# Expert stage of a fused attention and mixture-of-experts kernel: turning the gathered tokens with a DRAM scratch and VectorE block transposes in place of TensorE transposes

## The chip, the cores and the metric

One Trainium2 chip, one core of it. The time is that of the whole program on the device, in microseconds (us), and is the median of three runs. The engines are called as in the profile: PE is TensorE (PEld its weight loads), DVE is VectorE, ACT is ScalarE, POOL is GpSimd, SP is SyncE, which here issues the plain DMAs.

## The reference

Attention with keys and values averaged over groups of eight positions, followed by a mixture of eight experts of which each token uses one:

```python
k_p = k.reshape(B, H, Sp, 8, D).mean(axis=3)          # q, k, v: (8, 8, 576, 64) float32
v_p = v.reshape(B, H, Sp, 8, D).mean(axis=3)
attn = softmax(q @ k_p^T / sqrt(D));  attn_out = attn @ v_p
x = attn_out.transpose(0, 2, 1, 3).reshape(4608, 512)  # one row per token
logits = x @ w_gate + modality_bias[modality_id]       # (4608, 8)
e_idx = argmax(logits);  gate_w = softmax(logits)[e_idx]
for e in range(8):                                     # w1: (8, 512, 1024), w2: (8, 1024, 512)
    h = maximum(x[e_idx == e] @ w1[e], 0)
    out[e_idx == e] = gate_w * (h @ w2[e])
```

## The kernel before

The first part (up to about 195 us) computes the attention, writes each token's row to a DRAM table `xs`, and sorts the tokens by expert. A row of `xs` holds 512 numbers, the token's gate weight in column 512, and from column `RX` = 520 on one factor per head (8 of them) by which the 512 numbers have yet to be multiplied.

The second part works in slots of 256 tokens of one expert. There are `NSTAT` = 18 slots that always run (numbered s = 0 to 17 in the code; slot 5 of the title is s = 4), and more only if the experts' counts need them. Instructions are issued on each engine in the order in which the program writes them (`manual_schedule`).

While slot s is computed, slot s + 1 is prepared:

- `gather(s + 1, ...)`: two indirect DMAs on POOL fetch 128 token rows each into two of the four tiles `xg`. The transition into slot 17 fetches a third tile, `xe`, since the last slot there can hold 128 tokens more (its operand is `xw` and not one of the two `xhl`).
- `scale`: POOL multiplies the 512 numbers of each row by the head's factor (L153).
- `x_transposes`: four PE transposes per tile of 128 tokens put the 512 numbers on partitions, in PSUM tile `xt` (L168); ACT copies them to the high part of `xhl` in float32r (L170); DVE subtracts that from the original and writes the low part (L171). Products of float32 numbers are made from such high and low parts.

A slot has eight steps f = 0 to 7, one for each 128 columns of the hidden layer. Step f consists of

- `hidden(f)`, which calls `first_wide`: eight matmuls into PSUM tile `hp[f % 2]` (L188: high weights by high and low tokens, 512 columns; L191: low weights by high tokens, 256 columns). Then ACT copies half of `hp` to `ht` (L193), DVE adds the other half (L194), ACT makes `hh` = relu in float32r (L195), DVE makes the low part `hlo` (L197).
- `second(f - 1)`: the twelve matmuls of step f - 1 by w2 (L1248), from its `hh` and `hlo`, into `op`.
- `renew(f - 1)`: where the next slot has another expert, ACT (L136) and DVE (L139) split newly loaded weights into high and low parts; SP issues conditional loads of the weights of slot s + 2 (L126, L129; not moved where the expert stays the same). DVE's part and the loads are kept in the list `lag` and issued one or two steps later, between L195 and L197.

The last step ends with `close`: it issues the first matmuls of the next slot (`first_next`, which is step 0 of slot s + 1 and reads the high and low tokens of all its 256 columns), then `second(7)`. In step 0 of the next slot the outputs of the old one are multiplied by the gate weight (`evac`, L1219 on DVE, L1221 on ACT), and scattered to the output by POOL (L1225).

In the slots that matter here (s = 3 to 16), the gather is issued in step 0, `scale` in step 3, and `x_transposes` in step 5, with the third tile of the last transition in step 6:

```python
if f == (3 if EARLY_SLOTS <= s < NSTAT - 1 else 4) and nxt and not early:
    scale(s + 1, xg)
    ...
if f == (5 if EARLY_SLOTS <= s < NSTAT - 1 else 6) and nxt:
    x_transposes(s + 1, xg)
...
if f == NF - 1 and s != NSTAT - 2:
    close()
```

Of the kernel before, what the change touches and what calls it, by code (L numbers as in the profile page):

```python
# [9 lines left out]
F32 = mybir.dt.float32  # L10
# [5 lines left out]
ALU = mybir.AluOpType  # L16
# [6 lines left out]
P = 128  # L23
SLOT = 256
EARLY_GROUPS = 2
EARLY_SLOTS = 2
EXTRA = (128,)
OOB = 1 << 20


@with_exitstack
def kernel(
# [12 lines left out]
    nc = tc.nc  # L45
    ctx.enter_context(tc.manual_schedule(engines=ENGINES))
    B, H, S, HD = q.shape
    NTOK, D = out.shape
    E, _, FF = w1.shape
# [6 lines left out]
    NF = FF // P  # L56
    ND = D // P
    XW = D + 16
    RX = D + 8
    NSTAT = NTOK // SLOT  # L60
# [8 lines left out]
    dram = ctx.enter_context(tc.tile_pool(name="dram", bufs=1, space=bass.MemoryType.DRAM))  # L69
# [19 lines left out]
    xg = [cp.tile([P, XW], F32, name=f"xg{i}") for i in range(4)]  # L89
    gate = cp.tile([P, NT], F32, name="gate")  # L90
    tri = cp.tile([P, P], BF16, name="tri")
    xhl = [cp.tile([P, ND, 2, SLOT], F32R, name="xhl0")]
# [8 lines left out]
    sidx0 = cp.tile([P, 2 * EARLY_SLOTS], I32, name="sidx0")  # L101
    meta = cp.tile([1, 2 + 2 * (NSLOT + 1) + len(EXTRA)], I32, name="meta")
    meta0 = cp.tile([1, 1], I32, name="meta0")
# [10 lines left out]
    def load_regs(s, e_ap, c_ap):  # L114
        e = nc.values_load(e_ap, engines=SP_ENGINE, min_val=0, max_val=E - 1,
                           skip_runtime_bounds_check_because="a sum over at most one expert's index")
        c = None
        if c_ap is not None:
            c = nc.values_load(c_ap, engines=SP_ENGINE, min_val=0, max_val=1,
                               skip_runtime_bounds_check_because="a comparison's result")  # L120
        regs[s] = (e, c)
# [25 lines left out]
    def gather(s, idx, col, xgs, rows=NTOK):  # L147
        for tt in range(2):
            gather_tile(xgs[(2 * s + tt) % 4], idx, col + tt, rows)

    def scale_tile(x):
        xv = x[:, 0:D].rearrange("p (h d) -> p h d", h=H)
        nc.gpsimd.tensor_tensor(xv, xv, x[:, RX:RX + H].rearrange("p (h o) -> p h o", o=1).to_broadcast([P, H, HD]),  # L153
                                op=ALU.mult)

    def scale(s, xgs):
        for tt in range(2):
            scale_tile(xgs[(2 * s + tt) % 4])

    xw = None  # L160

    def x_transposes(s, xgs, tts=(0, 1)):
        ab = xhl[s % len(xhl)] if s != NSTAT - 1 else xw
        for tt in tts:
            x = xgs[(2 * s + tt) % 4] if tt < 2 else xgs[4]
            pt = ps_tr.tile([P, ND, P], F32, tag="tr", name=f"xt_{s}_{tt}")
            for d in range(ND):
                nc.tensor.transpose(pt[:, d, :], x[:, d * P:(d + 1) * P], ident)  # L168
            sl = slice(tt * P, (tt + 1) * P)
            nc.scalar.copy(ab[:, :, 0, sl], pt)  # L170
            nc.vector.tensor_sub(ab[:, :, 1, sl], pt, ab[:, :, 0, sl].bitcast(F32))  # L171
# [13 lines left out]
    def first_wide(f, ab, ph, t, hh, hlo, between=lambda: None):  # L185

        for d in range(ND):
            nc.tensor.matmul(ph, hl[f][:, 0, d * P:(d + 1) * P], ab[:, d, :, 0:SLOT],  # L188
                             start=(d == 0), stop=False)
        for d in range(ND):  # L190
            nc.tensor.matmul(ph[:, 0:SLOT], hl[f][:, 1, d * P:(d + 1) * P], ab[:, d, 0, 0:SLOT],  # L191
                             start=False, stop=(d == ND - 1))
        nc.scalar.copy(t, ph[:, SLOT:2 * SLOT])  # L193
        nc.vector.tensor_add(t, t, ph[:, 0:SLOT])  # L194
        nc.scalar.activation(hh, t, AF.Relu)  # L195
        between()
        nc.vector.scalar_tensor_tensor(hlo, t, 0.0, hh.bitcast(F32), op0=ALU.max, op1=ALU.subtract)  # L197
# [15 lines left out]
    with ExitStack() as actx:  # L213
# [586 lines left out]
        def finish_table(pt, n, go, so, nm):  # L800
# [6 lines left out]
                lambda: V.tensor_scalar(go, ix, -1.0, 0.0, op0=ALU.add, op1=ALU.max),  # L807
                lambda: V.tensor_scalar(lo, ix, 0.0, float(OOB), op0=ALU.is_equal, op1=ALU.mult),
                lambda: V.scalar_tensor_tensor(so, ix, -1.0, lo, op0=ALU.add, op1=ALU.add),
# [65 lines left out]
        for g in range(len(GROUPS) - 1):  # L875
            n = s1_of[2 * g + 1] + 2
# [74 lines left out]
        for n in range(N + 1):  # L951
            has, nxt, nxt2 = n < N, n + 1 < N, n + 2 < N
# [82 lines left out]
    mp = ctx.enter_context(tc.tile_pool(name="mp", bufs=1))  # L1035
# [3 lines left out]
    op = [[ps_op.tile([P, 512], F32, name=f"op{i}_{z}") for z in range(2)] for i in range(2)]  # L1039
    hp = [ps_hp.tile([P, 512], F32, name=f"hp{i}") for i in range(2)]  # L1040
    hts = [mp.tile([P, SLOT], F32, name=f"ht{i}") for i in range(2)]
    hhs = [mp.tile([P, SLOT], F32R, name=f"hh{i}") for i in range(2)]
    hlos = [mp.tile([P, SLOT], F32R, name=f"hlo{i}") for i in range(2)]
    CUT = 3
    xw = mp.tile([P, ND, 2, SLOT + P], F32R, name="xw")
# [3 lines left out]
    xe = xg[4]  # L1049
# [108 lines left out]
    ]  # L1158
    for i, r in enumerate(EXTRA):
        last_half += [  # L1160
# [31 lines left out]
    def do_late(s, f):  # L1192
        for fn in late.get((s, f), ()):
            fn()

    def slot_regs(s):
        load_regs(s, meta[0:1, 1 + s:2 + s], meta[0:1, 2 + NSLOT + s:3 + NSLOT + s])

# [6 lines left out]

    def part(s):

        ab = xhl[s % 2] if s != NSTAT - 1 else xw
        o = op[s % 2]
        third = op[(s + 1) % 2][0]  # L1210
        nxt, nxt2 = s + 1 < NSLOT, s + 2 < NSLOT
# [21 lines left out]
        def hidden(f, at=None, width=SLOT, **kw):  # L1233
            hh, hlo = at or (hhs[f % 2], hlos[f % 2])
            if width > SLOT:
                first(f, ab, hp[f % 2][:, 0:width], hh[:, 0:width], hlo[:, 0:width])()
            else:
                first_wide(f, ab, hp[f % 2], hts[f % 2], hh[:, 0:SLOT], hlo[:, 0:SLOT], **kw)
# [29 lines left out]

        def first_next():
            if nxt:  # L1270
                first_wide(0, xhl[(s + 1) % 2] if s + 1 != NSTAT - 1 else xw, hp[0], hts[0], hhs[0][:, 0:SLOT], hlos[0][:, 0:SLOT])

        def slot0(tail):
            for f in range(NF):
# [11 lines left out]
        def run(fs, tail):  # L1286
            later = []
            for f in fs:
                def pop():
                    if len(lag) > 1 or (f == 1 and lag):  # L1290
                        lag.pop(0)()
                if f:
                    hidden(f, between=pop)
                if f == 0:

                    if 0 < s < NSTAT - 1:
                        tail(later=later)
                    else:
                        tail()
                    if nxt and EARLY_SLOTS <= s < NSTAT - 1:  # L1300
                        gather(s + 1, gidx, 2 * (s + 1), xg)
                        if s == NSTAT - 2:
                            gather_tile(xe, gidx, 2 * NSTAT)
                if f == 0:
                    pop()
                do_late(s, f)
                if f == (0 if s >= EARLY_SLOTS else 1) and nxt and not early:
                    slot_flag(s + 1)
                if f == 0 and nxt2:
                    slot_regs(s + 2)  # L1310
                if s == 1 and f == 2:
                    gather(s + 1, gidx, 2 * (s + 1), xg)

                if s >= NSTAT - 1 and f == CUT and nxt:
                    gather(s + 1, gidx, 2 * (s + 1), xg)
                if f:
                    second(f - 1)
                    renew(f - 1)
                if f == (3 if EARLY_SLOTS <= s < NSTAT - 1 else 4) and nxt and not early:
                    scale(s + 1, xg)  # L1320
                    if s == NSTAT - 2:
                        scale_tile(xe)
                    while later:
                        later.pop(0)()
                if s == NSTAT - 2 and f == 4:
                    nc.gpsimd.drain()
                if f == (5 if EARLY_SLOTS <= s < NSTAT - 1 else 6) and nxt:
                    x_transposes(s + 1, xg)
                if s == NSTAT - 2 and f == 6:
                    x_transposes(s + 1, xg, (2,))  # L1330
                if f == NF - 1 and s != NSTAT - 2:
                    close()

# [64 lines left out]
    sl = mp.tile([P, 1], I32, name="sl")  # L1398
# [26 lines left out]
    def last_slots():  # L1425
# [9 lines left out]
                           skip_runtime_bounds_check_because="a sum over the one expert with the last slot")  # L1435
            for i in range(len(EXTRA))]

    def choose(i):
        if i == len(EXTRA):
            last_slots()  # L1440
            return
        with tc.If(fits[i] > 0) as cmp:
            kept = list(lag)
            parts[NSTAT - 1][5](EXTRA[i], parts[NSTAT - 2][4], tail)
            lag[:] = kept
        with cmp.Else():
            choose(i + 1)
# [35 lines left out]
```

## Time and profile before

| | |
|---|---|
| time, median of 3 runs (lowest to highest) | 610.44 us (609.77 to 613.24) |
| the profiled execution | 611.56 us, span 609.8 us |
| granted TensorE clock, mean over the span | 0.997 |
| busy: PE, PEld, DVE, ACT, POOL | 590.1, 512.3, 339.1, 273.1, 225.2 us |
| HBM read, written | 114.94 MB, 19.45 MB |

The span runs from the first to the last instruction of the profiled execution; its time lies around it. Busy times of different engines overlap. In the rows of the timeline the numbers are the start in us from the span's start, the duration in us, the engine, the line, the operation, the tile written and the tiles read, the shape, the count of instructions merged into the row, and in brackets the idle time of the engine before it with what ended that. In the rows of groups the number after the bar is the busy time in us, then the mean duration in ns.

### The profile page before, as it was taken

The numbers are of one execution on the slowest core, as the hardware profiler recorded it, in microseconds if no ns is written. First come the engines' busy times: TensorE is split into PE (matmuls) and PEld (weight loads), VectorE is DVE, ScalarE is ACT, GpSimd is POOL, SyncE is SP. The second block draws the span as 40 slices with busy tenths as digits, with TensorE's granted clock in tenths as the row PEclk, the third lists the DMA queues.
The fourth block names the chain that finished last, engine by engine and source line by source line (L and its number), as shares of the span: only waits on it lengthen the run. The fifth ranks groups of instructions, "written<-read, shape, count | busy, mean of one in ns | idle before, by whom it ended". The sixth has DMA issues, their size and how long they took to land.

```text
span 609.8 us, 12218 instructions
## 1 busy us (share of the span) xinstructions
PE 590.1 (97%) x3663; PEld 512.3 (84%) x3663; DVE 339.1 (56%) x815; ACT 273.1 (45%) x653; POOL 225.2 (37%) x325
## 2 busy tenths in 40 slices
PE   5899999999999999999999999999999999999996
PEld 4789889888898888888888888888888888888994
DVE  6757798789967556355344346643444476334311
ACT  3666576788551233333333346433333563333210
POOL 7789978664000142403313314304304224215101
PEclk9999899999999999999999999999999999999999
DMA  8999969983301911102102255102105611102001
GB/s 248 308 308 309 352 188 355 284 288 117 105 37 38 311 64 43 54 18 72 38 35 71 56 190 173 37 33 72 36 37 164 210 45 58 37 37 88 36 2 54
DMA packets 61104, 76.33 MB, mean 125 GB/s; under 512 B 15391, under 2 KB 39967, under 8 KB 61024
## 3 DMA queue, kind: packets, MB, share of 16 engines
q1 hardware_dynamic: 55104, 55.98, 29.5%
q0 software_dynamic: 5920, 19.44, 9.8%
q8 instruction: 31, 0.51, 0.4%
q14 instruction: 49, 0.40, 0.3%
HBM read 114.94 MB, written 19.45 MB: 220 GB/s over the span
## 4 chain that ended last, share of the span: by engine, by line
PE 78%; DVE 7%; POOL 5%; DMA 5%; ACT 2%; issue 2%; SPq 0%; POOLq 0%; DVEq 0%; ACTq 0%
PE op L1248 32%; PE hp L188 18%; PE hp L191 10%; DMA k<-in_k_dram 5%; PE av L640 3%; PE hp L178 3%; PE xt L168 2%; PE av L644 2%; PE sc L576 2%; PE ph L178 1%; PE pp L605 1%; POOL k L325 1%; PE pq L551 1%; DVE hl L139 1%; POOL v L325 1%
## 5 line engine op out<-in xcount | busy, mean ns | idle before, releaser
L1248 PE MATMUL op<-hl,hh 128*128 128x512 f32 x512 | 161.0, 396 | 0.0
L188 PE MATMUL hp<-xhl,hl 128*128 128x512 f32 x512 | 138.8, 393 | 0.0
L194 DVE TENSOR_TENSOR ht<-ht,hp 128x256 f32<-128x256 f32 x128 | 53.9, 421 | 124.3 <-ACT ht L193 121.2
L193 ACT COPY ht<-hp 128x256 f32<-128x256 f32 x128 | 47.8, 374 | 147.3 <-PE hp L191 145.4
L142 POOL DMA_INDIRECT xg<-xs,gidx x36 | 38.1, 1057 | 197.8 <-ACT ht L193 120.6
L188 PEld LDWEIGHTS hp<-xhl,hl 128*128 128x128 f32 x512 | 94.8, 188 | 19.2
L1248 PE MATMUL op<-hl,hlo 128*128 128x512 f32 x256 | 100.1, 391 | 0.2
L1248 PEld LDWEIGHTS op<-hl,hh 128*128 128x128 f32 x512 | 87.9, 190 | 11.3 <-ACT hh L195 0.3
L197 DVE SCALAR_TENSOR_TENSOR hlo<-ht,hh 128x256 fp32r<-128x256 f32 x128 | 63.3, 495 | 55.8 <-ACTq L1253 49.0
L191 PEld LDWEIGHTS hp<-xhl,hl 128*128 128x128 f32 x512 | 78.2, 189 | 10.3
L195 ACT ACTIVATE hh<-ht 128x256 fp32r<-128x256 f32 x128 | 53.6, 419 | 67.5 <-DVE ht L194 67.1
L191 PE MATMUL hp<-xhl,hl 128*128 128x256 f32 x512 | 81.2, 281 | 0.0
L1225 POOL DMA_INDIRECT out_dram<-ob,sidx x36 | 39.2, 1090 | 76.0 <-DMA out_dram<-ob,sidx 51.1
L1248 PEld LDWEIGHTS op<-hl,hlo 128*128 128x128 f32 x256 | 48.1, 188 | 12.6 <-DVE hlo L197 1.6
L640 PE MATMUL av<-vw,pt 128*128 128x146 f32 (+1 forms) x320 | 49.7, 294 | 1.9 <-ACT pt L610 1.1
L153 POOL TENSOR_TENSOR xg<-xg 128x512 f32<-128x512 f32 x32 | 35.5, 1115 | 32.4 <-DMA xg<-xs,gidx 32.2
L640 PEld LDWEIGHTS av<-vw,pt 128*128 128x128 f32 (+1 forms) x320 | 39.7, 180 | 4.1 <-ACT pt L610 2.2
L576 PE MATMUL sc<-kt,qt 128*128 128x144 f32 x256 | 37.3, 289 | 1.1 <-ACT qt L557 1.1
L576 PEld LDWEIGHTS sc<-kt,qt 128*128 128x128 f32 x256 | 33.1, 190 | 1.9 <-ACT qt L557 0.9
L583 DVE TENSOR_REDUCE mx<-sc 128x8 f32<-128x576 f32 (+1 forms) x40 | 27.7, 692 | 9.2 <-PE sc L576 6.8
L644 PE MATMUL av<-vw,pt 128*128 128x146 f32 (+1 forms) x160 | 31.1, 293 | 0.3
L139 DVE TENSOR_TENSOR hl<-raw,hl 128x1024 fp32r<-128x1024 f32 x24 | 29.0, 1219 | 0.4 <-issue 0.4
(261 smaller groups left out, 827.3 us busy)
## 6 DMA issues: line engine op xcount, KB each, us to landing
raw<-in_moe_w_dram SPq DMA_DIRECT2D x288, 256.0 KB
xs<-xb SPq DMA_DIRECT2D x16, 528.0 KB
k<-in_k_dram SPq DMA_DIRECT2D x7, 1024.0 KB
v<-in_v_dram SPq DMA_DIRECT2D x7, 1024.0 KB
q<-in_q_dram SPq DMA_DIRECT2D x7, 1024.0 KB
v<-in_v_dram SPq DMA_DIRECT2D x16, 128.0 KB
xs<-xb SPq DMA_DIRECT2D x8, 132.0 KB
k<-in_k_dram SPq DMA_DIRECT2D x4, 256.0 KB
```

What stands on the lines that cost most here:

```text
L142: nc.gpsimd.indirect_dma_start(out=x, out_offset=None, in_=xs[0:rows, :], in_offset=IndirectOffsetOnAxis(idx[:, col:col + 1].bitcast(U32), 0),
L188: nc.tensor.matmul(ph, hl[f][:, 0, d * P:(d + 1) * P], ab[:, d, :, 0:SLOT], start=(d == 0), stop=False)
L191: nc.tensor.matmul(ph[:, 0:SLOT], hl[f][:, 1, d * P:(d + 1) * P], ab[:, d, 0, 0:SLOT], start=False, stop=(d == ND - 1))
L193: nc.scalar.copy(t, ph[:, SLOT:2 * SLOT])
L194: nc.vector.tensor_add(t, t, ph[:, 0:SLOT])
L195: nc.scalar.activation(hh, t, AF.Relu)
L197: nc.vector.scalar_tensor_tensor(hlo, t, 0.0, hh.bitcast(F32), op0=ALU.max, op1=ALU.subtract)
L576: nc.tensor.matmul(dst, qt[:, i, :], kt[b % NB][:, :, h * SPL:(h + 1) * SPL], start=True, stop=True)
L640: nc.tensor.matmul(av[hs, u, 2 * VC * gg:2 * VC * (gg + 1)], pt[:, c, hs], vw[y][:, c].rearrange("p a x -> p (a x)"), start=(gg == 0), sto ...
L644: nc.tensor.matmul(dst4[hs], pt4[:, hs], v4[y][:, 2 * u:2 * u + 2, :], start=False, stop=True)
L1225: nc.gpsimd.indirect_dma_start(out=out[:, :], out_offset=IndirectOffsetOnAxis(idx.bitcast(U32), 0), in_=ob, in_offset=None, bounds_check=N ...
L1248: nc.tensor.matmul(ot, l[:, ts_], hl[f][:, w, D:2 * D], start=(f == 0 and n == 0), stop=(f == NF - 1 and n == 2))
```

## The change

For the slots s = 4 to 17 (`blocked(s)`: `FIRST_BLOCKED` = 4 up to `NSTAT`) `scale` and `x_transposes` are not called. In their place:

- step 3, `blocks_out`: for each tile of 128 tokens two DVE multiplications (128 x 256) do the scaling, and write the result in another order of columns into `xp`, a tile with two buffers; SP writes `xp` (256 KB) to a DRAM scratch `scr`. After all tiles, SP reads the scratch back with four DMAs, one for each group of 32 partitions, into `ys`, so that each 32 x 32 block of the tokens stands in the partitions that it will have when turned. The pieces read are 512 bytes long.
- step 5 + tt, `blocks_turn` for tile tt: one DVE instruction transposes all 32 x 32 blocks of the tile into `yt`, and ACT copies `yt` to the high part of the operand.
- step min(6 + tt, 7), `blocks_low`: DVE subtracts to make the low part, from `yt`.

`ys` and `yt` have one buffer each (they take the tags `bid` and `bsel` of tables used in earlier slots). Each of these stands in its step after `second(f - 1)` and `renew(f - 1)`, and in step 7 ahead of `close`.

```diff
+    scr = dram.tile([2, 3 * P, D], F32, name="scr")
+    ys = {}
+    NQ = P // QUAD
+
+    def blocks_out(s, xgs, tts):
+        for tt in tts:
+            x = xgs[(2 * s + tt) % 4] if tt < 2 else xgs[4]
+            xp = mp.tile([P, NQ, ND, QUAD], F32, tag="xp", bufs=2, name=f"xp_{s}_{tt}")
+            f = x[:, RX:RX + H].rearrange("p (k a o q) -> p k a o q", a=2, o=1, q=1)
+            for a in range(2):
+                nc.vector.tensor_tensor(
+                    xp[:, 2 * a:2 * a + 2].rearrange("p j k r -> p k j r"),
+                    x[:, 0:D].rearrange("p (k a j r) -> p a k j r", k=ND, a=2, j=2)[:, a],
+                    f[:, :, a].to_broadcast([P, ND, 2, QUAD]), op=ALU.mult)
+            nc.sync.dma_start(scr[s % 2, tt * P:(tt + 1) * P, :], xp.rearrange("p j k r -> p (j k r)"))
+        n = len(tts) * NQ
+        ys[s] = mp.tile([P, n, P], F32, tag="bid", name=f"y_{s}")
+        src = scr[s % 2, 0:len(tts) * P, :].rearrange("(u c) (j x) -> j c u x", c=QUAD, j=NQ)
+        for j in range(NQ):
+            nc.sync.dma_start(ys[s][j * QUAD:(j + 1) * QUAD], src[j])
+
+    yts = {}
+
+    def blocks_turn(s, tt):
+        yt = mp.tile([P, ND, P], F32, tag="bsel", name=f"yt_{s}_{tt}")
+        nc.vector.transpose(yt.rearrange("p k (u c) -> p u k c", c=QUAD),
+                            ys[s][:, NQ * tt:NQ * (tt + 1), :].rearrange("p u (k r) -> p u k r", r=QUAD))
+        ab = tokens_of(s)
+        nc.scalar.copy(ab[:, :, 0, tt * P:(tt + 1) * P], yt)
+        yts[s, tt] = yt
+
+    def blocks_low(s, tt):
+        ab = tokens_of(s)
+        sl = slice(tt * P, (tt + 1) * P)
+        nc.vector.tensor_sub(ab[:, :, 1, sl], yts[s, tt], ab[:, :, 0, sl].bitcast(F32))
+
+    def tts_of(s):
+        return (0, 1) if s != NSTAT - 1 else (0, 1, 2)
+
+    def blocked(s):
+        return FIRST_BLOCKED <= s < NSTAT
...
                 if f == (3 if EARLY_SLOTS <= s < NSTAT - 1 else 4) and nxt and not early:
-                    scale(s + 1, xg)
-                    if s == NSTAT - 2:
-                        scale_tile(xe)
+                    if blocked(s + 1):
+                        blocks_out(s + 1, xg, tts_of(s + 1))
+                    else:
+                        scale(s + 1, xg)
                     while later:
                         later.pop(0)()
...
-                if f == (5 if EARLY_SLOTS <= s < NSTAT - 1 else 6) and nxt:
+                if blocked(s + 1):
+                    for tt in tts_of(s + 1):
+                        if f == 5 + tt:
+                            blocks_turn(s + 1, tt)
+                        if f == min(6 + tt, NF - 1):
+                            blocks_low(s + 1, tt)
+                elif f == (5 if EARLY_SLOTS <= s < NSTAT - 1 else 6) and nxt:
                     x_transposes(s + 1, xg)
-                if s == NSTAT - 2 and f == 6:
-                    x_transposes(s + 1, xg, (2,))
                 if f == NF - 1 and s != NSTAT - 2:
                     close()
```

`tokens_of(s)` gives the operand of slot s (`xhl[s % 2]`, or `xw` for the last).

More of the change, by code (lines that the diff above doesn't have):

```diff
@@ L27 @@
 EXTRA = (128,)
+QUAD = 32
+FIRST_BLOCKED = 4
 OOB = 1 << 20
@@ L160, with tokens_of @@
     xw = None
+    def tokens_of(s):
+        return xhl[s % len(xhl)] if s != NSTAT - 1 else xw
     def x_transposes(s, xgs, tts=(0, 1)):
-        ab = xhl[s % len(xhl)] if s != NSTAT - 1 else xw
+        ab = tokens_of(s)
         for tt in tts:
@@ L1194, in do_late @@
             fn()
+    scr = dram.tile([2, 3 * P, D], F32, name="scr")
[26 more added lines that the diff above has]
+    def blocks_low(s, tt):
+        ab = tokens_of(s)
+        sl = slice(tt * P, (tt + 1) * P)
[4 more added lines that the diff above has]
+        return FIRST_BLOCKED <= s < NSTAT
     def slot_regs(s):
@@ L1206, in part @@
     def part(s):
-        ab = xhl[s % 2] if s != NSTAT - 1 else xw
+        ab = tokens_of(s)
         o = op[s % 2]
@@ L1270, in first_next @@
             if nxt:
-                first_wide(0, xhl[(s + 1) % 2] if s + 1 != NSTAT - 1 else xw, hp[0], hts[0], hhs[0][:, 0:SLOT], hlos[0][:, 0:SLOT])
+                first_wide(0, tokens_of(s + 1), hp[0], hts[0], hhs[0][:, 0:SLOT], hlos[0][:, 0:SLOT])
         def slot0(tail):
```

## The prediction

> **What bounds the kernel now.** I read the page first, then the groups of instructions from 330 us on, then the timeline of one slot, then DMA landings and the windows around the one place where the clock fell.
>
> ```profile
> span 609.8 us, 12218 instructions
> PE 590.1 (97%) x3663; PEld 512.3 (84%) x3663; DVE 339.1 (56%) x815; ACT 273.1 (45%) x653; POOL 225.2 (37%) x325
> PE   5899999999999999999999999999999999999996
> PEclk9999899999999999999999999999999999999999
> ...
> PE 78%; DVE 7%; POOL 5%; DMA 5%; ACT 2%; issue 2%; SPq 0%; POOLq 0%; DVEq 0%; ACTq 0%
> ```
>
> TensorE (PE) is full in every slice of the expert stage, at full clock. So time taken off its queue there comes off the end, and any stall of it is added. The timeline of one slot shows how tight its feeders are (columns: start, duration, engine, line; code steps f = 5, 6, 7, then f = 0 of the next slot):
>
> ```profile
> 420.48 1.07 PE L188 MATMUL hp<-xhl,hl 128*128 128x512 f32 x4
> ...
> 423.25 1.03 PE L168 MATMUL xt<-ident,xg 128*128 128x128 f32 x8
> 423.43 0.43 DVE L197 SCALAR_TENSOR_TENSOR hlo<-ht,hh 128x256 fp32r<-128x256 f32 x1 [0.48 <-ACTq L1253]
> ...
> 423.89 1.08 ACT L170 CAST xhl<-xt 128x512 fp32r<-128x512 f32 x2 [0.49 <-PE xt L168]
> ...
> 424.04 1.17 PE L188 MATMUL hp<-xhl,hl 128*128 128x512 f32 x4
> 424.51 1.29 DVE L171 TENSOR_TENSOR xhl<-xt,xhl 128x512 fp32r<-128x512 f32 x2 [0.65 <-ACT xhl L170]
> ...
> 426.89 1.07 PE L188 MATMUL hp<-xhl,hl 128*128 128x512 f32 x4
> ...
> 429.66 1.07 PE L188 MATMUL hp<-xhl,hl 128*128 128x512 f32 x4
> ...
> 431.30 0.37 ACT L193 COPY ht<-hp 128x256 f32<-128x256 f32 x1 [1.49 <-PE hp L191]
> ...
> 431.70 0.42 DVE L194 TENSOR_TENSOR ht<-ht,hp 128x256 f32<-128x256 f32 x1 [1.43 <-ACT ht L193]
> ...
> 432.16 0.42 ACT L195 ACTIVATE hh<-ht 128x256 fp32r<-128x256 f32 x1 [0.49 <-DVE ht L194]
> ...
> 432.43 1.07 PE L188 MATMUL hp<-xhl,hl 128*128 128x512 f32 x4
> 432.61 0.43 DVE L197 SCALAR_TENSOR_TENSOR hlo<-ht,hh 128x256 fp32r<-128x256 f32 x1 [0.48 <-ACTq L1253]
> ...
> 433.81 0.63 PE L1248 MATMUL op<-hl,hh 128*128 128x512 f32 x2
> ```
>
> The pitch of a step is 2.77 us (429.66 to 432.43). Its ACT-DVE chain L193, L194, L195, L197 ends 3.38 us after the step's first matmul (433.04 - 429.66), and the matmuls that need it start at 4.15 (433.81), their hlo part some 0.46 later. So the chain has about 1 us of slack.
>
> **What goes.** The step with the eight transposes lasts 3.56 us (420.48 to 424.04), and the next 2.85: 0.79 + 0.08 = 0.87 us over the pitch. Fourteen transitions lose them: -12.2, and four more transposes in the last one, -0.5: **-12.7 us**, all on TensorE. POOL's two scalings go too (L153 below); they end about two steps before L168 needs them, so nothing is gained by that itself.
>
> **The multiplications.** Four per slot on DVE at f = 3 (six before the last), 128x256 each; nearest row L194, 0.42 us, so 1.7 us.
>
> ```profile
> 438.12 1.04 POOL L153 TENSOR_TENSOR xg<-xg 128x512 f32<-128x512 f32 x1 [1.20 <-DMA xg<-xs,gidx]
> 438.14 1.29 DVE L197 SCALAR_TENSOR_TENSOR hlo<-ht,hh 128x256 fp32r<-128x256 f32 x1 [0.48 <-ACTq L1253]
> ...
> 439.59 1.04 POOL L153 TENSOR_TENSOR xg<-xg 128x512 f32<-128x512 f32 x1 [0.44 <-DMA xg<-xs,gidx]
> ...
> 440.91 0.43 DVE L197 SCALAR_TENSOR_TENSOR hlo<-ht,hh 128x256 fp32r<-128x256 f32 x1 [0.48 <-ACTq L1253]
> ```
>
> The gathers are in by 439.59, and hlo of f = 3 ends at 441.34 (call it T3), so DVE does not wait for them. DVE then idles 1.43 us until L194; 1.7 makes L194 0.3 late, inside the slack: nothing. (L197 stretched to 1.29 beside POOL's scaling; that goes, and was hidden.)
>
> **The scratch round trip.** SP issues two writes of 256 KB, waits until they have landed, then issues four reads of 512-byte pieces. No row shows SP's landing; these bound it:
>
> ```profile
> L1225 POOL DMA_INDIRECT out_dram<-ob,sidx x36: 974/1052/1986, 216.4 to 601.1; - x36
> DMA to landing us min/median/max: 2.5/2.9/4.8
> ```
> ```profile
> L142 POOL DMA_INDIRECT xg<-xs,gidx x36: 1000/1042/1253, 146.1 to 551.7; - x36
> DMA to landing us min/median/max: 3.4/3.8/6.9
> ```
> ```profile
> 360.14 0.39 SPq L126 DMA_DIRECT2D raw<-in_moe_w_dram  x1
> 360.83 0.34 SPq L129 DMA_DIRECT2D raw<-in_moe_w_dram  x1
> ```
> ```profile
> DMA  9321000000003341699999999799931000000000
> ```
> ```profile
> 164.62 1.08 SPq L680 DMA_DIRECT2D xs<-xb  x2
> ```
>
> Write: a scatter of 256 KB lands 2.9 - 1.05 = 1.85 us after its issue; with SP's 0.4 for the issue, 2.25. Read: the 40 tenth-slices from 360 us show the weight pair (512 KB) moving until about 363.1, 2.3 us after the second issue began. SP's issues are 0.55 apart (1.08 for two), so four reads land 3 x 0.55 + 2.2 + 0.2 = 4.05 after the first. Sum: T3 + 1.75 + 0.1 + 2.25 + 0.1 + 4.05 = T3 + 8.25. DVE reaches the first block turn at f = 5, after hlo of f = 5, T3 + 2 x 2.77 = T3 + 5.54. So it waits **L = 2.7 us**. By the ends of the rows (writes 1.5 to 3.8 after their issue, reads 3.0 to 5.5 in all) L is 1.2 to 4.7; I take the middle, as the queue is nearly empty in most slots.
>
> **What is queued behind the waits.** DVE is in order: behind the turn stands L194 of f = 6. ACT is in order: the copy of the turned block (0.6, as L170) stands ahead of L193 of f = 6. The second turn and its copy stand likewise ahead of f = 7, and the last subtraction (0.69) stands at f = 7 behind hlo, while the first matmul of the next slot reads its result. That makes one chain from landing to the next slot: turn, copy, L193, L194, L195, L197, subtraction, turn, copy, L193, L194, L195, L197, subtraction. A turn has no row; nearest is L171, a 128x512 DVE pass, 0.69 (half and double as ends). Sum: 0.69 + 0.6 + 1.64 + 0.69 + 0.69 + 0.6 + 1.64 + 0.69 = 7.25, with 14 handovers of 0.03: 7.7 us. TensorE would want that matmul 3 x 2.77 - 3.38 = 4.93 us after hlo of f = 5. Stall: L + 7.7 - 4.93 = **L + 2.8**; even with L = 0 it is 2.8. Less 0.87, each transition costs L + 1.9 = 4.6; thirteen, **+60 us**.
>
> By the Trainium skill (VectorE: DVE Perf Modes, The three transpose paths) a 128x128 bf16 turn takes 311 ns; four times that, an estimate, would be 1.24 a turn and add 2 x 0.55 x 14 = 15 us. No run here shows it yet.
>
> **SP's and POOL's queues.** On SP the weight loads of the next steps wait behind the reads, up to 4 us; a load has about a slot (22 us) until it is split, so 0. POOL loses work only.
>
> **The last transition.** The third tile's multiplication waits for a scratch buffer that the first write still reads (two buffers): DVE blocked to T3 + 4.1, third write landed at about 6.4, reads 4.6: landing T3 + 11.0, L = 5.5. At f = 7 another turn, copy and subtraction follow (2.0): 5.5 + 2.8 + 2.0 - 1.4 = **+9**.
>
> **Slots that change expert.** Two (16 of L139 from 330 us on):
>
> ```profile
> L139 DVE TENSOR_TENSOR hl<-raw,hl 128x1024 fp32r<-128x1024 f32 x16 | 19.5, 1219 | 0.4 <-issue 0.4
> ```
>
> L139 stands between L194 and L197, and lengthens each of two chain links by about 0.75, and delays the multiplications: 2 each, **+4**.
>
> **The clock.** A stall of 5.5 us splits: the matmuls after step 7's wait about 1.8 for f = 6's hh, run 1.4, then the rest, 3.7: 6.9 us with 1.4 busy.
>
> ```profile
> 66.46:69.88 3.42, 2.35 (x17) 2.11 (x17) 3.35 (x11) 2.11 (x8) 3.18 (x6) 1.00 1.06 360
> 69.88:73.29 3.41, 3.41 (x19) 2.67 (x19) 2.99 (x14) 1.16 (x5) 3.10 (x9) 0.50 1.04 338
> ...
> 602.36:605.77 3.41, 1.72 (x8) 1.10 (x6) 0.75 (x1) 0.00 (x0) 0.03 (x1) 1.00 0.25 91
> 605.77:609.18 3.41, 0.00 (x0) 0.00 (x0) 0.00 (x0) 0.00 (x0) 0.94 (x1) 1.00 0.18 68
> ```
>
> The granted clock fell to 0.50 for 3.41 us after a stretch in which TensorE was busy 2.35 of 3.42 us with small matmuls, and not after one of 1.72 of 3.41 with full ones. A stretch with at most 1.4 busy should lower it. Half clock for 3.41 us costs 1.7; fourteen times, **+24 us**.
>
> **Sum:** 60 + 9 + 4 + 24 = +97 (the removal is inside the 60 and the 9). The profiled execution took 611.6 us (span 609.8), 1.1 over the median of 610.44; on the median, **707 us**.
>
> **Rivals.**
> 1. The clock holds: TensorE's idle stretches stay below what lowers it. For it: 602.36 to 605.77 was half idle without a fall. Then 707 - 24 = 683. The Trainium skill (TensorE: Matmul & The Clock Gate, Why this matters for your kernels) says to avoid idle gaps of more than about 3 us, and that one idle window brings the half clock; by it 3.7 us would seldom hold a whole window. The fall at 69.88 came without such a gap, and the measurement decides.
> 2. The round trip is hidden (L = 0 to 0.5): shorter landings, SP's issues overlapping. The order at f = 6 and 7 still costs 1.9 to 2.4 a transition: 28 in the middle, +8 for the last and split slots, 4 of the clock term, as these stalls mostly stay short: 650.
> 3. Faster: DVE and ACT get through f = 6 and f = 7 inside TensorE's slack, so the last subtraction is done when the next slot's first matmul is due. Then only the -12.7 is left: 598. It decides where the stall is under 0.87, that is 2 us less than the chain with L = 0; the two turns would have to cost almost nothing. L194's 1.43 us of idle time speaks for it, the copies queued on ACT before L193 against it.
> 4. Transfers slower than I take them (32 partitions per read, behind weight loads): L = 4.7, 13 x 2 = 26 more, with 5 in the last: 738.
>
> **How the numbers follow.** Forecast 0.50, rival 1 0.20, rival 2 0.12, rival 3 0.04, rival 4 0.12, no change 0.02. Time: 707. The range reaches from rival 2 to rival 4, 648 to 738; turns at half or double their price (-10, +19) stay within it. Outside: rival 3, no change, half of rival 4 and some of rival 2. Faster by over 0.5% (about what a measurement of this kernel can tell from no change): 0.04; within: 0.02; slower: 0.94.
>
> **What would show it.** No L168 rows after slot 4; turns that wait on DMA for the reads, about 2.7 us; ACT's copy waiting for DVE; PE's wait before the first L188 of a slot, on the last subtraction, some 3 to 4 us; before it one of 1 to 2 us on hh; PEclk digits below 9 throughout. Wrong would be: reads landed before hlo of f = 5, a clock of 1.00 through the stalls, or the turns at another price than 0.69.

## The result and the profile after

The changed kernel takes 709.09 us (median of 4 runs, 708.93 to 712.28), against 611.79 us (609.77 to 613.24) for the kernel before: ratio 1.161, 95% interval 1.155 to 1.166. The profiled execution took 709.23 us, its span is 707.5 us; all spans below are those of profiled executions (before: 609.8).

The page of the changed kernel, to be laid beside that of before:

```profile
span 707.5 us, 12209 instructions
PE 613.4 (87%) x3547; PEld 521.7 (74%) x3547; DVE 369.0 (52%) x902; ACT 271.9 (38%) x653; POOL 192.6 (27%) x296
...
PE   6999999999999996887978879797796977979596
PEclk9999999999999997998979799899999999999899
```

TensorE was full in every slice of the expert stage. Of the 25 slices from the first changed transition on, it is now busy less than 90% in 17 (PE digit below 9), and its mean clock is below 0.9 in six (PEclk digit below 9). It has 116 matmuls fewer and 23 us more busy time: the same matmuls ran longer. No other engine has become full.

One quiet transition (no weights moving) in the timeline. L1228 is the block turn, L1231 the copy of its result to the high part, L1237 the subtraction, L198 to L202 the four links that were L193 to L197, L193 and L196 the first matmuls of a step, L1297 those by w2:

```profile
444.14 0.42 DVE L202 SCALAR_TENSOR_TENSOR hlo<-ht,hh 128x256 fp32r<-128x256 f32 x1 [0.48 <-ACTq L1302]
...
446.97 0.71 DVE L1228 STREAM_TRANSPOSE yt<-y 128x512 f32<-128x512 f32 x1 [2.40 <-DMA y<-scr]
...
447.71 0.62 ACT L1231 CAST xhl<-yt 128x512 fp32r<-128x512 f32 x1 [3.61 <-DVE yt L1228]
448.24 0.37 ACT L198 COPY ht<-hp 128x256 f32<-128x256 f32 x1
...
449.56 0.74 PE L1297 MATMUL op<-hl,hh 128*128 128x512 f32 x2 [1.29 <-ACTq L1302]
...
449.88 0.68 DVE L1237 TENSOR_TENSOR xhl<-yt,xhl 128x512 fp32r<-128x512 f32 x1
...
450.60 0.71 DVE L1228 STREAM_TRANSPOSE yt<-y 128x512 f32<-128x512 f32 x1
...
451.35 0.62 ACT L1231 CAST xhl<-yt 128x512 fp32r<-128x512 f32 x1 [1.84 <-DVE yt L1228]
451.87 0.36 ACT L198 COPY ht<-hp 128x256 f32<-128x256 f32 x1
...
453.51 0.68 DVE L1237 TENSOR_TENSOR xhl<-yt,xhl 128x512 fp32r<-128x512 f32 x1
454.34 2.05 PE L193 MATMUL hp<-xhl,hl 128*128 128x512 f32 x4 [3.12 <-DVE xhl L1237]
```

VectorE waits 2.40 us for the reads. From there each row starts when the one before it ends: turn, copy, the links of step 6, subtraction, turn, copy, the links of step 7, subtraction, and only then the next slot's first matmul, 7.37 us after the landing (446.97 to 454.34). TensorE stands idle twice, 1.29 and 3.12 us. The four matmuls of L193 then take 2.05 us where they took 1.07. The windows around them show why: the granted clock is 0.50 (columns: length, busy time with count of PE, PEld, DVE, ACT, POOL, then granted clock, DMA share, GB/s):

```profile
446.83:453.66 6.83, 3.10 (x15) 2.06 (x13) 3.78 (x8) 2.61 (x6) 0.00 (x0) 1.00 0.00 0
453.66:460.49 6.83, 6.15 (x17) 5.04 (x18) 2.08 (x4) 1.44 (x3) 0.45 (x1) 0.50 0.01 2
460.49:467.32 6.83, 6.83 (x37) 5.89 (x36) 1.69 (x4) 1.75 (x6) 3.59 (x4) 1.00 0.39 119
```

The three waits over the whole stage, summed (us in total, times, longest):

```profile
DVE yt L1228 <- DMA y<-scr: 47.5, 14, 5.2
...
PE hp L193 <- DVE xhl L1237: 37.2, 13, 3.7
...
PE op L1297 <- ACTq L1302: 29.6, 12, 4.1
```

So three terms make the loss, and they are those of the forecast: a wait for the DRAM trip, a chain through the in-order queues behind it, and half clock after the stalls. The experiments price each by itself.

### The profile page after: what moved, and what is told of

The parts are those of the page before. It is cut to its first block, busy times and chain, and to the rows that moved or that the text cites. A ratio compares the mean times of both kernels' runs of the same rounds, so it can differ in the third digit from the quotient of the medians.

```text
span 707.5 us, 12209 instructions
## 1 busy us (share of the span) xinstructions
PE 613.4 (87%) x3547; PEld 521.7 (74%) x3547; DVE 369.0 (52%) x902; ACT 271.9 (38%) x653; POOL 192.6 (27%) x296
## 3 DMA queue, kind: packets, MB, share of 16 engines
HBM read 122.54 MB, written 27.05 MB: 211 GB/s over the span
## 5 line engine op out<-in xcount | busy, mean ns | idle before, releaser
L1297 PE MATMUL op<-hl,hh 128*128 128x512 f32 x512 | 174.5, 424 | 34.3 <-ACTq L1302 29.6
L193 PE MATMUL hp<-xhl,hl 128*128 128x512 f32 x512 | 146.1, 409 | 37.2 <-DVE xhl L1237 37.2
L193 PEld LDWEIGHTS hp<-xhl,hl 128*128 128x128 f32 x512 | 99.4, 197 | 64.8 <-issue 35.7
L1297 PEld LDWEIGHTS op<-hl,hh 128*128 128x128 f32 x512 | 95.1, 205 | 49.8 <-ACTq L1302 32.1
L1297 PE MATMUL op<-hl,hlo 128*128 128x512 f32 x256 | 105.6, 412 | 0.6 <-DVE hlo L202 0.6
L198 ACT COPY ht<-hp 128x256 f32<-128x256 f32 x128 | 47.4, 370 | 150.4 <-PE hp L196 149.4
L196 PEld LDWEIGHTS hp<-xhl,hl 128*128 128x128 f32 x512 | 82.6, 199 | 11.2
L196 PE MATMUL hp<-xhl,hl 128*128 128x256 f32 x512 | 85.2, 291 | 0.0
L202 DVE SCALAR_TENSOR_TENSOR hlo<-ht,hh 128x256 fp32r<-128x256 f32 x128 | 55.0, 430 | 55.5 <-ACTq L1302 50.7
L1297 PEld LDWEIGHTS op<-hl,hlo 128*128 128x128 f32 x256 | 51.9, 203 | 15.0 <-DVE hlo L202 2.9
L1231 ACT CAST xhl<-yt 128x512 fp32r<-128x512 f32 x26 | 16.1, 618 | 80.5 <-DVE yt L1228 80.5
L1228 DVE STREAM_TRANSPOSE yt<-y 128x512 f32<-128x512 f32 x29 | 20.6, 711 | 48.0 <-DMA y<-scr 47.5
```

Source lines behind the costliest of these rows:

```text
L1297: nc.tensor.matmul(ot, l[:, ts_], hl[f][:, w, D:2 * D], start=(f == 0 and n == 0), stop=(f == NF - 1 and n == 2))
```

## Experiments

Two theories stand against each other. The **chain theory** is that of the prediction. The **round-trip theory** says that the DRAM trip alone costs. A third, the **load theory**, says that the added VectorE and ScalarE work does.

### The trip taken away

```diff
-            nc.sync.dma_start(scr[s % 2, tt * P:(tt + 1) * P, :], xp.rearrange("p j k r -> p (j k r)"))
+            ys[s, tt] = xp                                  # of which there are three buffers now
...
-        for j in range(NQ):
-            nc.sync.dma_start(ys[s][j * QUAD:(j + 1) * QUAD], src[j])
...
-                            ys[s][:, NQ * tt:NQ * (tt + 1), :].rearrange("p u (k r) -> p u k r", r=QUAD))
+                            ys[s, tt])
```

> The turn reads the scaled tile straight from SBUF; the scratch write and the four reads are left out (so the blocks are turned but stay in their partition groups), everything else stands where it stood. Chain theory (turns, copies and subtractions stand in the in-order queues of VectorE and ScalarE ahead of the next steps' work): with the wait for the reads at zero a transition still stalls TensorE 2.8 us, the last 4.8, the two slots that change expert 2 more each: 45 us of idle time, less 12.7 for the transposes, and 5 to 20 of half clock: about 656 us (648 to 668). Round-trip theory (the DRAM trip is what costs): no stall is left, the transposes are saved, 599 us (595 to 606).

Measured: 652.28 us, ratio 1.068 (1.065 to 1.071). This kernel leaves out the move of the blocks between groups of partitions, so its output is another; TensorE and VectorE execute as many instructions as in the changed kernel (3547 and 902). Without any DMA between, some 42 of the 97 us stay, so the round-trip theory falls. Three transitions in the timeline, and a pair of 3.41 us windows for each:

```profile
272.55 1.16 PE L193 MATMUL hp<-xhl,hl 128*128 128x512 f32 x4 [3.48 <-DVE xhl L1232]
...
477.53 1.17 PE L193 MATMUL hp<-xhl,hl 128*128 128x512 f32 x4 [2.20 <-DVE xhl L1232]
...
503.71 1.17 PE L193 MATMUL hp<-xhl,hl 128*128 128x512 f32 x4 [2.21 <-DVE xhl L1232]
```
```profile
267.42:270.83 3.41, 1.65 (x9) 1.05 (x7) 1.94 (x4) 1.31 (x3) 0.00 (x0) 1.00 0.00 0
270.83:274.25 3.42, 1.70 (x9) 1.53 (x10) 1.35 (x5) 0.00 (x0) 0.00 (x0) 1.00 0.00 0
475.63:479.04 3.41, 1.51 (x9) 1.36 (x10) 1.27 (x3) 0.42 (x1) 0.00 (x0) 1.00 0.00 0
479.04:482.45 3.41, 3.41 (x11) 2.65 (x10) 1.54 (x3) 1.47 (x3) 0.49 (x1) 0.50 0.01 2
...
499.52:502.93 3.41, 1.98 (x11) 1.38 (x9) 1.94 (x5) 1.31 (x3) 0.00 (x0) 1.00 0.55 154
502.93:506.34 3.41, 2.63 (x14) 2.28 (x15) 1.05 (x3) 0.42 (x2) 0.00 (x0) 1.00 0.52 154
```

Only the second stall is left, 2.2 us in quiet slots, on the last subtraction (L1232 here). And the clock fell after some of these stalls and not after others: after the second of the three, and not after the first, which is longer, nor after the third, which is as long.

### The stalls filled with other matmuls

```diff
+                if f == NF - 1 and blocked(s + 1):
+                    ft = ps_tr.tile([P, 2 * SLOT], F32, tag="tr", name=f"ft_{s}")
+                    filler(ft, 6)          # matmuls of this slot's tokens by themselves, 128x512
                 if f:
                     second(f - 1)
                     renew(f - 1)
+                if f == NF - 1 and blocked(s + 1):
+                    filler(ft, 13)
```

> As the changed kernel, with matmuls whose result nobody reads put on TensorE in step 7: 6 ahead of the matmuls of step 6, 13 ahead of the first matmuls of the next slot (0.23 us each), so that they fall into the two stalls. Clock theory (half clock after the stalls costs some 35 us): the clock stays at 1.00, 709 - 35 = 674 us (668 to 684), although TensorE has 266 matmuls more to do. Rival (the clock falls where TensorE has nothing to do anyway, and the chain sets the time): no gain, 707 to 715 us.

Measured: 685.40 us, ratio 1.124 (1.120 to 1.127); granted clock over the span:

```profile
core 0: 683.2 us, clock 1.000
```
```profile
441.48 1.17 PE L193 MATMUL hp<-xhl,hl 128*128 128x512 f32 x4 [0.20 <-DVE xhl L1237]
...
468.45 1.16 PE L193 MATMUL hp<-xhl,hl 128*128 128x512 f32 x4 [0.18 <-DVE xhl L1237]
```

266 useless matmuls make the kernel 23.7 us faster (709.09 - 685.40): the clock term. The clock theory holds against its rival, but its number was too high: the expectation had got 35 us by taking the idle times in brackets, some 75 us in all, from the loss and the saved transposes (97 + 13), and the brackets understate a stall. The pitch of a quiet slot is the better measure: 468.45 - 441.48 = 26.97 us (27.05 to 27.16 in the other five quiet slots), against 8 x 2.77 = 22.16 without transposes or stalls, is a stall of 4.81, where the brackets of the changed kernel above add up to 4.41. Over fourteen transitions that is about 6 of the 11 us too many; the rest is not assigned.

### Half of the tokens

```diff
-        return (0, 1) if s != NSTAT - 1 else (0, 1, 2)
+        return (0,)                                          # blocks for the first 128 tokens only
...
+                    if f == 5:
+                        x_transposes(s + 1, xg, (1,))        # scaled by GpSimd in step 3, as before
```

> Only the first 128 tokens of a slot go through the scratch and VectorE (turn in step 5, subtraction in step 6); the second 128, and the third tile of the last slot, are scaled by GpSimd and transposed on TensorE in step 5 (6) as before. Chain theory: the chain has one link and ends two steps before the next slot; the reads, half as long, land about 1.3 us after VectorE gets there, TensorE stalls 0.2 to 0.5 a transition, saves 0.43: 611 us (604 to 620), clock 0.99 or more. Round-trip theory: writing, landing and reading back last nearly as long for half the bytes, so more than half of the loss stays: 650 to 690 us.

Measured: 634.32 us, ratio 1.038 (1.035 to 1.042): between the two, and a miss for both. The timeline gives the transition that the chain theory had worked out, and others that it had not:

```profile
439.22 0.71 DVE L1228 STREAM_TRANSPOSE yt<-y 128x512 f32<-128x512 f32 x1 [1.31 <-DMA y<-scr]
...
442.63 0.74 PE L1297 MATMUL op<-hl,hh 128*128 128x512 f32 x2 [0.59 <-ACTq L1302]
```
```profile
487.23 0.71 DVE L1228 STREAM_TRANSPOSE yt<-y 128x512 f32<-128x512 f32 x1 [2.69 <-DMA y<-scr]
```
```profile
490.63 0.73 PE L1297 MATMUL op<-hl,hh 128*128 128x512 f32 x2 [1.96 <-ACTq L1302]
```

```profile
DVE yt L1228 <- DMA y<-scr: 27.4, 14, 2.9
```

The first pair is the quiet case: a wait of 1.31 us, a stall of 0.59, and no second stall, since the chain ends a step earlier; by itself it would give the 611 expected. But the mean wait is 27.4 / 14 = 1.96 us, for two reasons seen in the traces. In transitions beside weight loads the writes land late: the first read is issued 3.89 us after the write in the second case (479.78 to 483.67), and 2.57 us after it in the quiet one (433.07 to 435.64). And now and then one issue on SP lasts longer; in the changed kernel (SP's issues; min, median, max in ns):

```profile
L1216 SPq DMA_DIRECT2D scr<-xp x29: 320/354/1652, 258.8 to 648.1; - x29
```
```profile
L1221 SPq DMA_DIRECT2D y<-scr x56: 318/442/1857, 261.5 to 651.6; - x56
```

TensorE's stalls add up to some 19 us and the clock is at 0.990 in place of 0.997, which is at most about 4 us (0.7% of 633); less 6 for the transposes saved, 17 of the 23 us more span are accounted for, and the rest is not assigned. What the run does show: with one chain link in place of two and half of the bytes, most of the loss is gone (24 us are left of 97) although the trip is still there, with 1.96 us of waiting in place of 3.4 in the mean.

### Each turn twice

```diff
-        nc.vector.transpose(yt.rearrange("p k (u c) -> p u k c", c=QUAD),
-                            ys[s][:, NQ * tt:NQ * (tt + 1), :].rearrange("p u (k r) -> p u k r", r=QUAD))
+        for _ in range(2):
+            nc.vector.transpose(yt.rearrange("p k (u c) -> p u k c", c=QUAD),
+                                ys[s][:, NQ * tt:NQ * (tt + 1), :].rearrange("p u (k r) -> p u k r", r=QUAD))
```

> The changed kernel with every block turn issued twice into the same tile (29 more VectorE instructions of 0.71 us). Chain theory: both turns of a transition stand in the chain that ends at the next slot's first matmul, the last transition has three: 29 x 0.71 = 20.6 us more, and a little of half clock: 730 us (726 to 738). Rival (VectorE is half idle, and the transitions wait for the DRAM trip alone, so a turn on data that has landed is hidden): 709 to 713 us.

Measured: 737.16 us (731.50 to 739.68), ratio 1.203 (1.195 to 1.212): 28 us over the changed kernel's 709. The 20.6 of the chain fit in it: by the pages TensorE's idle time (span less busy time) grew by 18.3 us, from 94.1 to 112.4. Its busy time grew by 9.1 us for the same matmuls, as the clock fell to 0.918 over the span (0.944 before the doubling). A turn on VectorE, half idle as it is, is paid in full where it stands in the chain. The rival is out.

### Scaling and writing a step earlier

```diff
-                    if blocked(s + 1):
-                        blocks_out(s + 1, xg, tts_of(s + 1))
-                    else:
+                    if not blocked(s + 1):
                         scale(s + 1, xg)
...
+                if f == 2 and blocked(s + 1):
+                    blocks_out(s + 1, xg, tts_of(s + 1))
```

> The changed kernel with scaling, writing and reading back in step 2 in place of step 3, turns and subtractions where they were. Chain theory: the trip starts up to 2.77 us earlier less about 1 us that VectorE then waits for the gather, so the wait of 2.4 us before the first turn falls to about 0.7 in quiet slots, and each transition keeps its 2.2 to 2.8 us of chain: between the 652 us of the kernel without the trip and 709, near 670 (660 to 682). Round-trip theory: the wait gone, most of the loss gone: 600 to 625 us.

Measured: 674.62 us, ratio 1.104 (1.096 to 1.111). The wait before the first turn fell as expected, from 2.40 to about 0.7 us in quiet transitions (10.8 us in all, where it was 47.5), and the chain stayed, by TensorE's wait for the last subtraction (39.5 us, where it was 37.2):

```profile
428.56 0.71 DVE L1228 STREAM_TRANSPOSE yt<-y 128x512 f32<-128x512 f32 x1 [0.66 <-DMA y<-scr]
```
```profile
PE hp L193 <- DVE xhl L1237: 39.5, 13, 3.8
...
DVE yt L1228 <- DMA y<-scr: 10.8, 10, 2.8
```

### One slot ahead

```diff
-FIRST_BLOCKED = 4
+FIRST_BLOCKED = 6                  # up to slot NSTAT - 2; the others by x_transposes
...
                     if nxt and EARLY_SLOTS <= s < NSTAT - 1:
-                        gather(s + 1, gidx, 2 * (s + 1), xg)
+                        if not blocked(s + 1):
+                            gather(s + 1, gidx, 2 * (s + 1), xg)
+                        if blocked(s + 2):
+                            gather(s + 2, gidx, 2 * (s + 2), xg)
...
-                        if f == 5 + tt:
+                        if f == 1 + 2 * tt:
                             blocks_turn(s + 1, tt)
-                        if f == min(6 + tt, NF - 1):
+                        if f == 2 + 2 * tt:
                             blocks_low(s + 1, tt)
...
+                if f == 5 and blocked(s + 2):
+                    blocks_out(s + 2, xg, (0, 1))
+                    keep_gates(s + 2)                        # GpSimd copies the gate columns
```

> Slots s = 6 to 16 are gathered, scaled, written and read back one slot earlier (scaling and scratch in step 5 of slot s - 2), and turned in slot s - 1 with one piece a step: turn 0 in step 1, subtraction in step 2, turn 1 in step 3, subtraction in step 4; gates are copied to tiles of their own by GpSimd. Slots 4, 5 and 17 are as before the change. The same round trip, the same VectorE and ScalarE work, only other places in the queues. Chain theory: each piece delays its step's feeders by 0.4 us, inside the slack of 1 us; 11 transitions save 0.87 each, the two slots with split weights lose 1 each: 604 us (600 to 609). Load theory (the added VectorE and ScalarE work itself costs): a loss stays, 630 us or more.

Measured: 603.06 us (median of 6 runs, 601.10 to 604.12) against 610.33 for the kernel before on the same chip: ratio 0.9885 (0.9863 to 0.9906), 1.2% faster. The page and a turn in the timeline:

```profile
PE   5899999999999999999999999999999999999996
...
PEclk9999999999999999999999999999999999999999
```
```profile
428.89 1.07 PE L193 MATMUL hp<-xhl,hl 128*128 128x512 f32 x4
...
429.78 0.71 DVE L1228 STREAM_TRANSPOSE yt<-y 128x512 f32<-128x512 f32 x1
...
430.52 0.62 ACT L1231 CAST xhl<-yt 128x512 fp32r<-128x512 f32 x1 [1.49 <-DVE yt L1228]
...
431.05 0.36 ACT L198 COPY ht<-hp 128x256 f32<-128x256 f32 x1
...
431.65 1.07 PE L193 MATMUL hp<-xhl,hl 128*128 128x512 f32 x4
```

The block turn of 0.71 us and its copy delay L198 as they do in the changed kernel, but in a step whose slack takes it: TensorE's pitch stays 2.76 us (428.89 to 431.65), and the turn waits for no DMA. The same trip and the same work per token, other places in the queues, and the loss has become a gain; the load theory falls.

### One slot ahead, each turn twice

The doubling of the turns above, in the kernel one slot ahead.

> The kernel with slots 6 to 16 turned one slot ahead, each turn issued twice (22 more VectorE instructions of 0.71 us). Chain theory: a turn in a step of its own delays the feeders by 0.4 us, a second one by 0.7 more, 1.1 against about 1 us of slack: 0 to 0.3 us a turn, 1 to 8 us in all, 604 to 611 us, far below the 20.6 us that the same doubling costs where the turns stand in the chain. Load theory (VectorE work costs wherever it stands): 22 x 0.71 = 15.6 us more, 619 us.

Measured: 607.43 us (604.74 to 608.72), ratio 0.993 (0.990 to 0.996). That is 4.4 us over the single turn (2.6 by the two ratios), for 22 turns more, at most 0.2 us each in the mean; in the chain the doubling cost 28 us for 29, about 1 each. Rows of a step beside split weights, and of one in a quiet slot:

```profile
368.97 1.08 PE L193 MATMUL hp<-xhl,hl 128*128 128x512 f32 x4
...
371.13 0.73 PE L1305 MATMUL op<-hl,hh 128*128 128x512 f32 x2 [0.62 <-ACT hh L200]
...
373.19 1.08 PE L193 MATMUL hp<-xhl,hl 128*128 128x512 f32 x4
```
```profile
413.94 1.45 DVE L1229 STREAM_TRANSPOSE yt<-y 128x512 f32<-128x512 f32 x2
...
416.07 1.07 PE L193 MATMUL hp<-xhl,hl 128*128 128x512 f32 x4
...
418.84 1.07 PE L193 MATMUL hp<-xhl,hl 128*128 128x512 f32 x4
```

The mean hides two cases. In most quiet steps the doubled turn costs nothing: the pitch stays 2.77 us (416.07 to 418.84). In four steps beside the splitting of weights, which takes from the same slack, the pitch is 4.22 (368.97 to 373.19), 4.02, 4.17 and 4.02 us, against 2.95, 3.19, 2.96 and 3.31 with the single turn; these four alone add 4.0 us.

## Why the prediction was right

**The transposes.** 0.87 us a transition off TensorE's queue: right. With the stalls out of the way, 11 transitions should save 9.6. From the step with the transposes into slot s = 5 to the one into the last slot, which both kernels have, the profiled executions took 277.22 us before (282.04 to 559.26) and 268.04 one slot ahead (280.66 to 548.70): 9.2 less. By the times 7.3 were measured (610.33 - 603.06); what takes back the rest outside of that stretch is not shown.

**The multiplications.** Four in 1.43 us (1.7 forecast), hidden as said: the step's pitch does not change.

**The wait for the trip.** Forecast 2.7 us: about right for the six quiet transitions, which waited 2.38 to 2.45, and too low for the seven others, which waited 3.29 to 4.79; the last waited 5.25 (5.5 forecast). The thirteen before the last have a mean of (47.5 - 5.25) / 13 = 3.25, so this term was 0.55 us a transition too small. The landing was split otherwise than forecast: the reads were issued at T3 + 3.5, not 4.2, and took 4.5 us, not 4.05; the two errors nearly cancel. The prediction took the nearly empty queue as the rule, and did not count slow issues on SP.

**The chain.** 7.37 us where 7.7 was forecast; a turn is 0.71 (0.69 forecast by L171's row). The forecast's eight terms add up to 7.24 and not 7.25, which changes nothing. Each of its links shows in the rows, and the doubled turns price two of them. The estimate of 1.24 a turn, four times the figure for a 128x128 bf16 turn in the Trainium skill (VectorE: DVE Perf Modes, The three transpose paths), was too high.

**The sum without the clock.** The filled kernel has the stalls at full clock: 683.2 - 609.8 = 73.4 us, against 60 + 9 + 4 = 73. In part that is luck: longer waits in seven transitions against a shorter chain in all. A quiet transition costs 4.81 - 0.87 = 3.9 us (up to 4.1), not 4.6. A slot that changes expert was forecast to cost 2 us more than the others; in the filled kernel the step with its stall lasts 10.0 and 10.1 us, where 7.5 to 7.7 are usual in quiet slots: 2.4 us, of which 0.7 is a longer wait for the reads.

**The clock.** That half clock would follow the stalls was right; that the forecast of 24 us meets the measured 23.7 is luck. The forecast was fourteen falls of 3.41 us, 48 us in all, with TensorE busy throughout. Half clock in fact lasted some 75 us more than before, by the mean clocks (0.944 over 707.5 us, 0.997 over 609.8). It came after thirteen of the fourteen transitions, for 6.83 us in two of them (the one shown above is one) and 10.24 us in three. In part of it TensorE was idle (from 269.34 to 276.17, 6.83 us at half clock, it was busy for 1.57 + 1.64), and so it cost 23.7 and not half of 75. Nor were the PEclk digits below 9 throughout, as forecast, but in six of 25 slices. And the stretch that the forecast began from does not give a limit: no share of busy time separates the falls (see the last section). Rival 1, the clock holding, is out: it would have been 683, and the filled kernel, which is that case, took 685.

The kernel without the trip has ten gaps of 2.2 to 2.4 us, and half clock after five of them, while one gap of 3.48 us brought no fall; in all, eight of its fourteen transitions lost the clock. So the rule of the Trainium skill (TensorE: Matmul & The Clock Gate, Why this matters for your kernels), to avoid gaps of more than about 3 us, is not enough here.

**Rival 2** (the trip hidden, 650) is the kernel without the trip, 652. **Rival 3**, the faster end, needed the chain out of the next slot's way, as one slot ahead it is; nothing in the change itself did that. **Rival 4**, a wait of 4.7 us in every transition, came near in three only (4.33, 4.36 and 4.79).

## What to carry to other kernels

Work moved from a full engine to half-idle ones is free only by its place: on engines that execute in order, each instruction put ahead of the full engine's feeders eats their slack (here 1 us a step), and an operand finished in the last step before its use has none. So follow a moved operand from its landing to the first instruction that reads it, and count every row in each queue on the way; if that is longer than the time there is, start it a stage earlier rather than make it faster. A short stall can cost more through the clock, here 23.7 us on top of 73; filling it with useless matmuls shows how much.

## What the runs showed of the hardware

- Whether a stall lowers the clock depends on where it falls in time, and not on its length alone. The falls lie on a grid of 3.41 us (those at 427.84 and 479.04 in the kernel without the trip are 51.20 us apart, 15 steps). There a stall of 2.20 us that lay nearly whole in one stretch of this grid (1.51 us of TensorE work in it) was followed by 3.41 us at 0.50; one of 2.21 us that was split over two (1.98 and 2.63 us of work) was not, nor was one of 3.48 us (1.65 and 1.70). The busy time of a stretch does not settle it: in the changed kernel one with 1.50 us kept the clock, and before the change one with 2.35 us of small matmuls lost it. What else counts is not shown.

```profile
593.61:597.02 3.41, 1.50 (x9) 1.14 (x7) 0.89 (x2) 0.89 (x2) 0.00 (x0) 1.00 0.14 25
597.02:600.43 3.41, 1.65 (x6) 0.98 (x6) 1.98 (x4) 1.29 (x3) 0.00 (x0) 1.00 0.00 0
```

- One issue of a DMA on SP can last 1.65 or 1.86 us, where the median is 0.35 to 0.44. Two transitions of the changed kernel that have such an issue (on SP from 586.59 and 619.40), and no weights moving, waited 3.77 and 3.75 us for the reads, against 2.4 in the other quiet ones.
- The block transpose of a 128x512 float32 tile takes 0.711 us, with hardly any scatter (711 to 715 ns), about as long as a subtraction over the same tile (0.68).
- Four reads of 128 KB in pieces of 512 bytes took 4.5 us from the first issue to landing in a quiet slot (SP issues from 442.49, landing by 446.97), of which 1.8 us are the issues.
